# Low parts of layer 2 on VectorE, weight sums among the block products, and weight pieces spread over four periods

## The chip, the core and the metric

One core of a Trainium2 chip runs the whole program. The metric is the device time of one execution in microseconds (us); lower is better. TensorE multiplies (its operands come from SBUF, its sums go to PSUM), VectorE (DVE), ScalarE (ACT) and GpSimd (POOL) work elementwise, and SyncE (SP) issues nearly all DMAs. Each engine takes its instructions strictly in order.

## The reference

Pooled attention, then two mixture-style layers on 2304 tokens of width 512:

```python
x = attention(pooled q, k, v)            # 2304 x 512
h = x @ w1_in;  g = h - tanh(h);            x = g @ w1_out
h = x @ w2_in;  g = h * sigmoid(1.702 * h); out = g @ w2_out
# w_in: 512 x 2048, w_out: 2048 x 512, float64 in memory
```

## The kernel before

**High and low parts.** TensorE multiplies in fp32r. To keep accuracy every operand is split into a high part, a rounded copy that ScalarE makes (`activation(..., Copy)`), and a low part, the value less its high part, which VectorE or GpSimd subtracts. Each product is then three: high x high, high x low, low x high. A low part waits for its high part, and so its engine waits for ScalarE.

**Weights.** Weights come as pieces of 128 x 512 float64, loaded by SP into two alternating buffers `raw` and converted bit by bit: `convert_steps` is `shift` (L137 on ScalarE, L138 on VectorE), `sign` (L144), `flush` (L151) and `tail` (L158) on VectorE, then `split` (high L165 on ScalarE, low L166 on GpSimd). 'i' pieces are of w_in, 'o' pieces of w_out.

**Order.** The schedule is written by hand: lists of jobs are hung on named places (`at(step, place, job)`) and run there, so the program order of each engine's queue is the order in which the places are passed.

**Stages.** Attention runs to about 395 us. `moe` then goes through 50 steps: 40 for layer 1 (four quarters of w_in's columns, five token blocks, two halves each) and steps 40 to 49 for the first quarter of layer 2, the *plain quarter*. A step n issues `h_part(n)` (24 products of 512 or 384 columns into one PSUM tile), `y_part(n - 2)` (products of g and w_out, 18 or 24 a step) and `gate(n)`: `split_g(n - 1)` (high part L1070 on ScalarE, low part L1072), in layer 2 a sigmoid on ScalarE (L1127) and the product h * s on VectorE (L1131), and the accumulations of earlier y (VectorE L1175, ScalarE L1173). Places of a step are "start", "split", "convert", "end". PSUM has four tiles in rotation, so TensorE waits where an older tile has not been read.

In the plain quarter the operands of the rest are prepared beside the steps: `split_x` (L106, L110) for the plain blocks; `combine` (L705) forms sums X1 to X4 of token blocks, `stage` splits them (high L712, low L714) in one of two buffers and sends them to DRAM (L715); `keep` sends raw operands there (L733); `fetch` brings all back later (L737). `prepared` converts w_in pieces and sends them to a home (L759) or splits w_out pieces (L765, L766); `form` combines w_in pieces to sums S1 to S4 (L789) and splits these (high L800, low L803).

`second_layer` does the other three quarters of layer 2 with Winograd-style block products: nine periods i (three quarters by three token groups; a quarter's index s). A period has seven block products of 24 matmuls each (L915, places h0 to h6, PSUM banks a, b, c in turn), each followed by `h_after` (VectorE L927 to L938, which frees banks), the gate (L943, L944), and then the six products of the previous period's g with w_out (L967, places y0 to y5, 12 matmuls each) with accumulations `add` on VectorE (L980). `low_g` (L953) makes the low part of g on GpSimd. w_in pieces of a quarter are formed at y0 of the quarter before; pieces are loaded and converted at the places that `plan` and `loads` give.

Of the kernel before, what the change touches and what calls it, by code (L numbers as in the profile page):

```python
# [9 lines left out]
I32 = mybir.dt.int32  # L10
# [13 lines left out]
def f32(ap):  # L24
    return ap.bitcast(F32)
# [3 lines left out]
def tile_pooled_attention_two_moe(  # L29
# [94 lines left out]
            nc.sync.dma_start(out=raw.rearrange("p (a b) -> p a b", a=shape), in_=src)  # L124
        return raw

    def convert_steps(raw, hi, lo, shape, box, to=None):
        def shift():
            box["t"] = to
            if to is None:  # L130
                box["t"] = wpool.tile([128, DM], I32, tag="wt", name="wt", bufs=2)
            if raw.dtype == F32:
                nc.scalar.activation(f32(box["t"][:]), raw, AF.Copy)
                return
            top = raw[:, :, 1]
            box["a"] = wpool.tile([128, DM], F32, tag="wa", name="wa", bufs=1)
            nc.scalar.activation(box["a"], f32(top), AF.Abs)  # L137
            nc.vector.tensor_scalar(  # L138
                out=box["t"], in0=top, scalar1=3, scalar2=0x3FFFFFF8,
                op0=ALU.logical_shift_left, op1=ALU.bitwise_and,  # L140
            )

        def sign():
            nc.vector.scalar_tensor_tensor(  # L144
                out=box["t"], in0=raw[:, :, 1], scalar=-0x40000000, in1=box["t"],
                op0=ALU.bitwise_and, op1=ALU.bitwise_or,
            )

        def flush():
            t, a = box["t"], box["a"]  # L150
            nc.vector.scalar_tensor_tensor(  # L151
                out=f32(t[:]), in0=a, scalar=2.0 ** -15 * 1.125, in1=f32(t[:]),
                op0=ALU.is_ge, op1=ALU.mult,
            )

        def tail():
            t = box["t"]
            nc.vector.scalar_tensor_tensor(  # L158
                out=t, in0=raw[:, :, 0], scalar=29, in1=t,
                op0=ALU.logical_shift_right, op1=ALU.bitwise_or,  # L160
            )

        def split():
            t = f32(box["t"][:]).rearrange("p (a b) -> p a b", a=shape)
            nc.scalar.activation(hi, t, AF.Copy)  # L165
            nc.gpsimd.tensor_tensor(lo, t, f32(hi), op=ALU.subtract)  # L166

        def nothing():
            pass

        bits = [sign, flush, tail] if raw.dtype == I32 else [nothing] * 3
        return [shift, *bits, split]
# [6 lines left out]
    def piece(kind, n):  # L179

        li, f = divmod(n, NQ * 4)
        if kind == "i":
            src = layers[li][0][f].rearrange("p (c f) -> p c f", c=NKC)
            shape = NKC
        else:
            src = layers[li][1][f * 128:(f + 1) * 128, :].rearrange("p (a d) -> p a d", a=1)
            shape = 1
        box = {}

        def ld():  # L190
            box["raw"] = load_piece(src, shape)

        def cv(j):
            def go():
                if "s" not in box:
                    w = weight(kind, n)
                    hi, lo = ((w[:, :, 0, :], w[:, :, 1, :]) if kind == "i"
                              else (w[:, 0:1, :], w[:, 1:2, :]))
                    box["s"] = convert_steps(box["raw"], hi, lo, shape, box)
                box["s"][j]()  # L200
            return go

        return [ld] + [cv(j) for j in range(5)]
# [432 lines left out]
    def second_layer(mem, HL, work, TEMPS):  # L636
# [73 lines left out]
        def stage(n, o, m):  # L710
            t = stages[m]
            nc.scalar.activation(t[:, 0], shed[o], AF.Copy)  # L712
            eng = nc.vector if o in (X3, X4) else nc.gpsimd
            eng.tensor_tensor(t[:, 1], shed[o], f32(t[:, 0]), op=ALU.subtract)  # L714
            nc.sync.dma_start(out=kept[n][o], in_=whole(t))  # L715

        def keep(n, o):
# [21 lines left out]
        def prepared(kind, qn, f, home=None):  # L739
            n = qn * 4 + f  # L740
            m = n - NQ * 4
            if kind == "i":
                src, shape = layers[1][0][m].rearrange("p (c f) -> p c f", c=NKC), NKC
            else:
                src = layers[1][1][m * 128:(m + 1) * 128, :].rearrange("p (a d) -> p a d", a=1)
                shape = 1
            box = {}

            def ld():
                box["raw"] = load_piece(src, shape)  # L750

            def cv(js):
                def go():
                    if "s" not in box:
                        box["s"] = convert_steps(box["raw"], None, None, shape, box)
                    for j in js:
                        box["s"][j]()
                    if js[-1] == 3 and home is not None:
                        nc.sync.dma_start(out=home, in_=f32(box["t"][:]))  # L759
                return go  # L760

            def split():
                w, t = weight("o", n), f32(box["t"][:]) if home is None else home
                t = t.unsqueeze(1)
                nc.scalar.activation(w[:, 0:1, :], t, AF.Copy)  # L765
                nc.gpsimd.tensor_tensor(w[:, 1:2, :], t, f32(w[:, 0:1, :]), op=ALU.subtract)  # L766

            return [ld, cv((0, 1)), cv((2, 3)), split], box

        def form(qn, fp, boxes, homes):  # L770
# [29 lines left out]
                nc.scalar.activation(w[:, a:b + 1, 0], source(a, b), AF.Copy)  # L800

            def low(a, b):
                nc.gpsimd.tensor_tensor(  # L803
                    w[:, a:b + 1, 1], source(a, b), f32(w[:, a:b + 1, 0]), op=ALU.subtract)

            def run(fn, *args):
# [17 lines left out]
        def early(w, place, *js):  # L824
            opening.extend((w, place, j) for j in js)
# [8 lines left out]
        for qn in range(QN, 2 * NQ):  # L834
# [8 lines left out]
            if s == 0:  # L843
                for n in range(4):
                    early(1 + n, "end", ins[n][0][0])
                    early(3 + n, "convert", ins[n][0][1])
                    early(3 + n, "end", ins[n][0][2])
                early(7, "start", *fs[0])
                early(8, "start", *fs[1])
                for n in range(3):  # L850
                    early(5 + n, "end", outs[n][0])
                    early(7 + n, "convert", outs[n][1], outs[n][2])
                early(7, "end", outs[0][3])
                early(8, "end", outs[1][3], outs[3][0])
                plan = ((outs[3], 0, "h3", "h4"),)
                loads = []
            elif s == 1:
                plan = (
                    (ins[0][0], 1, "h4", "h5"), (ins[1][0], 1, "y1", "y2"),
                    (ins[2][0], 1, "y3", "y4"), (ins[3][0], 2, "h0", "h1"),  # L860
                    (outs[0], 2, "h3", "h4"), (outs[1], 2, "y1", "y2"),
                    (outs[2], 2, "y3", "y4"), (outs[3], 3, "h2", "h3"))
                at(2, "h5", outs[0][3])
                at(2, "y3", outs[1][3])
                loads = list(zip((
                    (0, "h5"), (0, "h6"), (1, "h6"), (1, "y3"), (1, "y5"), (2, "h2"), (2, "h5"),
                    (2, "y3")), (js[0] for js, *_ in plan), strict=True))
            else:
                plan = (
                    (ins[0][0], p, "h5", "h6"), (ins[1][0], p, "y2", "y3"),  # L870
                    (ins[2][0], p + 1, "h0", "h1"), (ins[3][0], p + 1, "h3", "h4"),
                    (outs[0], p + 1, "y1", "y2"), (outs[1], p + 2, "h0", "h1"),
                    (outs[2], p + 2, "h3", "h4"), (outs[3], p + 2, "y2", "y3"))
                at(p + 1, "y4", outs[0][3])
                loads = list(zip((
                    (p, "h0"), (p, "h2"), (p, "h5"), (p, "y3"), (p + 1, "h2"), (p + 1, "h5"),
                    (p + 1, "y3"), (p + 2, "h2")), (js[0] for js, *_ in plan), strict=True))
            for js, i, one, two in plan:
                at(i, one, js[1])
                at(i, two, js[2])  # L880
            for place, job in loads:
                at(*place, job)
            if s > 0:
                if s > 1:
                    at(p + 2, "h5", outs[1][3])
                at(p + 2, "y0", *fs[0], *fs[1])
            q = s * NG
            at(q + 1, "h3", outs[2][3])
            at(q + 1, "h4", outs[3][3])
# [135 lines left out]
    def moe(ctx: ExitStack, ending):  # L1025
# [38 lines left out]
        def split_g(n):  # L1064
            b = steps[n][2]
            at = TEMPS[f"g{n % 2}"]
            gt = mem[:, at:at + 4 * TB].rearrange("p (j r t) -> p j r t", j=2, r=2)
            gt = gt[:, :, :, 0:TBS[b]]
            g = gg.pop(n)
            nc.scalar.activation(gt[:, :, 0, :], g, AF.Copy)  # L1070
            eng = nc.gpsimd if n < len(steps) - 1 else nc.vector
            eng.tensor_tensor(gt[:, :, 1, :], g, f32(gt[:, :, 0, :]), op=ALU.subtract)  # L1072
            gs[n] = gt

# [206 lines left out]
```

## Time and profile before

| | us |
|---|---|
| median of 3 runs | 1204.1 (1200.88 to 1204.54) |
| the profiled execution | 1201.35 |
| its span in the trace | 1199.6 |

| engine | busy us | share of the span |
|---|---|---|
| TensorE matmul | 1180.7 | 98% |
| TensorE weight load | 982.3 | 82% |
| VectorE | 987.5 | 82% |
| ScalarE | 644.0 | 54% |
| GpSimd | 599.6 | 50% |

Busy shares are means over the stages. An engine that waits inside an instruction (for a port or a clock) counts as busy, so a high share alone does not say that it does useful work all that time. The profile has, beside the page with these sums, windows (busy time of each engine in a stretch), timelines, the chain of waits that ended last, and groups of instructions by line.

### The profile page before, as it was taken

To read this page: it belongs to the slowest core of one execution; us is meant where nothing else is said; L and a number is where in the kernel's file an instruction comes from. 1 tells how busy PE (TensorE), PEld (TensorE's weight loads), DVE (VectorE), ACT (ScalarE), POOL (GpSimd) and SP (SyncE) were. 2 spreads that over 40 slices of the span, in tenths; PEclk is the share of its full clock that TensorE was granted. 3 is DMA by queue.
4 is the path that set the end of the run, shared out by engine and by line. 5 is a ranking of instruction groups with operands and counts; after the bars stand their busy time and mean duration, and the time that the engine had idled before them with its cause. 6 is when DMAs were issued, how large, how long until landed. Compare 5 with 4: busy or idle time off the path is not lost. (4 is left out here: it accounts for less than half of the span.)

```text
span 1199.6 us, 23548 instructions
## 1 busy us (share of the span) xinstructions
PE 1180.7 (98%) x9492; PEld 982.3 (82%) x9492; DVE 987.5 (82%) x1115; ACT 644.0 (54%) x955; POOL 599.6 (50%) x388
## 2 busy tenths in 40 slices
PE   9999999999999999999999999998989998999998
PEld 7777676767676888888898898897879997999996
DVE  6788888888888799999999999989975998787442
ACT  4656565656565678676666666664544343333220
POOL 6888888788877323333323323333451354335221
PEclk9999999999999999999999999998999999999999
DMA  4222322233221021110110111113988667665512
GB/s 150 98 89 77 144 82 90 89 122 107 81 81 50 12 63 36 54 53 36 53 53 36 36 53 36 36 36 149 337 330 340 247 238 278 264 229 193 202 41 100
DMA packets 50156, 143.91 MB, mean 120 GB/s; under 512 B 13184, under 2 KB 18816, under 8 KB 50048
## 3 DMA queue, kind: packets, MB, share of 16 engines
q1 hardware_dynamic: 49504, 142.01, 32.7%
q8 instruction: 75, 1.23, 0.4%
q10 hardware_dynamic: 544, 0.39, 0.1%
q14 instruction: 33, 0.27, 0.1%
HBM read 116.13 MB, written 21.31 MB: 115 GB/s over the span
## 5 line engine op out<-in xcount | busy, mean ns | idle before, releaser
L338 DVE TENSOR_REDUCE mt<-mx 128x2 fp32r<-128x1024 f32 (+2 forms) x176 | 195.8, 1136 | 59.9 <-PE mx L326 37.1
L413 POOL TENSOR_TENSOR sum<-sum,pf 128x576 f32<-128x576 f32 x126 | 185.0, 1468 | 9.9
L402 ACT ACTIVATE pf<-sc 128x576 f32<-128x576 f32 x288 | 173.8, 653 | 22.5 <-PE sc L396 10.8
L1155 PE MATMUL y<-mem,big 128*128 128x512 f32 (+1 forms) x780 | 184.8, 368 | 0.9 <-POOL mem L1072 0.9
L1155 PEld LDWEIGHTS y<-mem,big 128*128 128x128 f32 x780 | 142.6, 188 | 20.5 <-POOL mem L1072 1.6
L1072 POOL TENSOR_TENSOR mem<-work,mem 128x1024 fp32r<-128x1024 f32 (+1 forms) x49 | 109.8, 2242 | 87.9 <-ACT mem L1070 87.8
L428 PE MATMUL acc<-pf,v 128*32 128x288 f32 x2304 | 146.3, 407 | 0.0
L1058 PE MATMUL h<-mem,big 128*128 128x512 f32 (+1 forms) x564 | 127.1, 377 | 0.0
L166 POOL TENSOR_TENSOR big<-wt,big 128x512 fp32r<-128x512 f32 x33 | 45.0, 1363 | 161.4 <-ACT big L165 153.3
L428 PEld LDWEIGHTS acc<-pf,v 128*32 128x32 f32 x2304 | 71.6, 110 | 65.7 <-ACT pf L402 4.5
L1058 PEld LDWEIGHTS h<-mem,big 128*128 128x128 f32 x564 | 104.3, 188 | 17.0
L953 POOL TENSOR_TENSOR mem<-work,mem 128x768 fp32r<-128x768 f32 x24 | 46.7, 1959 | 143.1 <-ACT mem L948 131.9
L967 PE MATMUL y<-big,mem 128*128 128x512 f32 x405 | 114.0, 390 | 0.0
L1120 ACT ACTIVATE work<-work 128x1024 f32<-128x1024 f32 (+1 forms) x40 | 39.1, 977 | 107.6 <-DVE work L1118 107.6
L396 PE MATMUL sc<-qh,kh 64*128 64x288 f32 x576 | 91.5, 314 | 0.0
L967 PEld LDWEIGHTS y<-big,mem 128*128 128x128 f32 x405 | 75.9, 188 | 15.6
L445 ACT ACTIVATE u<-acc 128x576 f32<-128x576 f32 x30 | 19.6, 652 | 125.6 <-PE acc L437 125.6
L396 PE MATMUL sc<-row,sel 64*128 64x288 f32 x576 | 85.0, 291 | 0.3 <-ACT row L373 0.3
L396 PE MATMUL sc<-qh,kl 64*128 64x288 f32 x576 | 85.0, 291 | 0.0
L396 PE MATMUL sc<-ql,kh 64*128 64x288 f32 x576 | 84.8, 291 | 0.0
L1058 PE MATMUL h<-mem,w 128*128 128x512 f32 (+1 forms) x376 | 84.7, 377 | 0.0
L1058 PEld LDWEIGHTS h<-mem,w 128*128 128x128 f32 x376 | 69.6, 188 | 11.4
(167 smaller groups left out, 2644.1 us busy)
## 6 DMA issues: line engine op xcount, KB each, us to landing
mem<-x SPq DMA_DIRECT2D x36, 768.0 KB
big<-x SPq DMA_DIRECT2D x27, 768.0 KB
raw<-in_moe_w_in_dram SPq DMA_DIRECT2D x32, 512.0 KB
raw<-in_moe_w_out_dram SPq DMA_DIRECT2D x32, 512.0 KB
v<-in_v_dram SPq DMA_DIRECT2D x16, 576.0 KB
x<-big SPq DMA_DIRECT2D x12, 768.0 KB
kr<-in_k_dram SPq DMA_DIRECT2D x15, 576.0 KB
qr<-in_q_dram SPq DMA_DIRECT2D x15, 576.0 KB
```

The source lines that it names most:

```text
L166: nc.gpsimd.tensor_tensor(lo, t, f32(hi), op=ALU.subtract)
L338: nc.vector.tensor_reduce(out, src, AX.X, ALU.max, negate=True)
L396: nc.tensor.matmul(sc[:, s, 0:HB], w[r], m[r, xs], start=(n == 0), stop=(n == 3))
L402: nc.scalar.activation(pf, sc[:, :, 0:HB], AF.Exp, scale=SCALE)
L413: nc.gpsimd.tensor_add(out, parts[p, x], new)
L428: nc.tensor.matmul(acc[32 * n:32 * n + 32, 0], pairs[p]["v"][:, s, t, 32 * h:32 * h + 32], new[t][:, s, :], start=(t == 0), stop=(t == KT ...
L953: eng.tensor_tensor(g[:, :, 1], halves[n][:, fp], f32(g[:, :, 0]), op=ALU.subtract)
L967: nc.tensor.matmul(y, gts[2 * side + fp][:, j, r, 128 * t:128 * t + 128], wo[:, p, :], start=(k == 0), stop=(k == len(terms) - 1))
L1058: nc.tensor.matmul(hb[:, j, 0:TBS[b]], wi[:, c, w, :], x[r][c], start=(k == 0), stop=(k == 3 * NKC - 1))
L1072: eng.tensor_tensor(gt[:, :, 1, :], g, f32(gt[:, :, 0, :]), op=ALU.subtract)
L1120: nc.scalar.activation(a, u, AF.Relu, bias=-T2)
L1155: nc.tensor.matmul(ys[m][:, 0:w], lhsT, rhs, start=(fp == 0 and not low and j == p == 0), stop=(fp == 1 and low and j == 1))
```

## The change

- The low parts that GpSimd made in the plain quarter go to VectorE: of g (`split_g` for layer 2), of `stage` (X1 and X2; X3 and X4 were there), of 'o' pieces from the third of the plain quarter on (`convert_steps` gets `eng`), of `prepared` and of `form`. `low_g` in the block periods stays on GpSimd, as do layer 1's low parts.
- The weight sums of `form` (L789) move from y0 of a quarter's last period to h2 and h4 of that period; the high and low parts stay at y0.
- The load of the plain quarter's last prepared w_out piece moves from the end of step 48 to that of step 49.
- The conversions of each further quarter's eight pieces are spread from some three periods over four, with other places for their loads and for the splits of the first two 'o' pieces.

```diff
-    def convert_steps(raw, hi, lo, shape, box, to=None):
+    def convert_steps(raw, hi, lo, shape, box, eng=None):
...
-            nc.gpsimd.tensor_tensor(lo, t, f32(hi), op=ALU.subtract)
+            (eng or nc.gpsimd).tensor_tensor(lo, t, f32(hi), op=ALU.subtract)
...
-                    box["s"] = convert_steps(box["raw"], hi, lo, shape, box)
+                    late = nc.vector if kind == "o" and n >= NQ * 4 + 2 else None
+                    box["s"] = convert_steps(box["raw"], hi, lo, shape, box, late)
...
         def stage(n, o, m):
             t = stages[m]
             nc.scalar.activation(t[:, 0], shed[o], AF.Copy)
-            eng = nc.vector if o in (X3, X4) else nc.gpsimd
-            eng.tensor_tensor(t[:, 1], shed[o], f32(t[:, 0]), op=ALU.subtract)
+            nc.vector.tensor_tensor(t[:, 1], shed[o], f32(t[:, 0]), op=ALU.subtract)
...
-                nc.gpsimd.tensor_tensor(w[:, 1:2, :], t, f32(w[:, 0:1, :]), op=ALU.subtract)
+                nc.vector.tensor_tensor(w[:, 1:2, :], t, f32(w[:, 0:1, :]), op=ALU.subtract)
...
             def low(a, b):
-                nc.gpsimd.tensor_tensor(
+                nc.vector.tensor_tensor(
                     w[:, a:b + 1, 1], source(a, b), f32(w[:, a:b + 1, 0]), op=ALU.subtract)
...
-                early(8, "end", outs[1][3], outs[3][0])
+                early(8, "end", outs[1][3])
+                early(9, "end", outs[3][0])
                 plan = ((outs[3], 0, "h3", "h4"),)
                 loads = []
-            elif s == 1:
-                plan = (
-                    (ins[0][0], 1, "h4", "h5"), (ins[1][0], 1, "y1", "y2"),
-                    (ins[2][0], 1, "y3", "y4"), (ins[3][0], 2, "h0", "h1"),
-                    (outs[0], 2, "h3", "h4"), (outs[1], 2, "y1", "y2"),
-                    (outs[2], 2, "y3", "y4"), (outs[3], 3, "h2", "h3"))
-                at(2, "h5", outs[0][3])
-                at(2, "y3", outs[1][3])
-                loads = list(zip((
-                    (0, "h5"), (0, "h6"), (1, "h6"), (1, "y3"), (1, "y5"), (2, "h2"), (2, "h5"),
-                    (2, "y3")), (js[0] for js, *_ in plan), strict=True))
             else:
-                plan = (
-                    (ins[0][0], p, "h5", "h6"), (ins[1][0], p, "y2", "y3"),
-                    (ins[2][0], p + 1, "h0", "h1"), (ins[3][0], p + 1, "h3", "h4"),
-                    (outs[0], p + 1, "y1", "y2"), (outs[1], p + 2, "h0", "h1"),
-                    (outs[2], p + 2, "h3", "h4"), (outs[3], p + 2, "y2", "y3"))
...
+                if s == 1:
+                    plan = (
+                        (ins[0][0], 0, "y1", "y2"), (ins[1][0], 1, "h4", "h5"),
+                        (ins[2][0], 1, "y1", "y2"), (ins[3][0], 1, "y3", "y4"),
+                        (outs[0], 2, "h5", "h6"), (outs[1], 2, "y4", "y5"),
+                        (outs[2], 3, "h2", "h3"), (outs[3], 3, "h5", "h6"))
+                    whens = ((0, "h0"), (0, "h5"), (0, "y3"), (1, "h6"), (1, "y3"), (1, "y5"),
+                             (2, "y1"), (3, "h0"))
+                    ends = (2, "y3"), (3, "h1")
+                else:
+                    plan = (
+                        (ins[0][0], p, "y1", "y2"), (ins[1][0], p, "y3", "y4"),
+                        (ins[2][0], p + 1, "h1", "h2"), (ins[3][0], p + 1, "h4", "h5"),
+                        (outs[0], p + 1, "y2", "y3"), (outs[1], p + 2, "h5", "h6"),
+                        (outs[2], p + 2, "y4", "y5"), (outs[3], p + 3, "h2", "h3"))
...
             if s > 0:
-                if s > 1:
-                    at(p + 2, "h5", outs[1][3])
-                at(p + 2, "y0", *fs[0], *fs[1])
+                at(p + 2, "h2", fs[0][0])
+                at(p + 2, "h4", fs[1][0])
+                at(p + 2, "y0", *fs[0][1:], *fs[1][1:])
...
-            eng = nc.gpsimd if n < len(steps) - 1 else nc.vector
+            eng = nc.gpsimd if steps[n][0] == 0 else nc.vector
             eng.tensor_tensor(gt[:, :, 1, :], g, f32(gt[:, :, 0, :]), op=ALU.subtract)
```

In a line of `plan`, (piece, period, one, two), the first two bit operations of a piece run at place `one` of that period and the last two at `two`; p is the first period of the quarter before.

## Rows read from the trace of the kernel before

**Rows 1.** Windows: us; busy us (count) of PE, PEld, DVE, ACT, POOL; clock; DMA share; GB/s.

```profile
816.90:824.00 7.10, 7.07 (x19) 5.58 (x20) 6.89 (x9) 3.09 (x5) 2.44 (x2) 0.57 0.17 65
...
1007.30:1194.80 187.50, 187.44 (x925) 167.20 (x923) 113.47 (x142) 53.20 (x72) 60.22 (x34) 1.00 0.50 188
...
829.50:906.60 77.10, 73.33 (x331) 61.73 (x329) 64.26 (x71) 40.85 (x62) 37.90 (x19) 0.98 0.91 339
```

**Rows 2.** Chain that ended last, in order of time: start us, us, what.

```profile
900.06 6.49 DMA big<-x
...
940.10 16.36 PE y L967 x72
...
958.57 2.08 PE b L915 x12
```

**Rows 3.** Timeline of TensorE from 808 us: start us, us, what [idle before <-releaser].

```profile
808.16 5.64 PE L1058 MATMUL h<-mem,big 128*128 128x512 f32 x24
816.93 7.20 PE L1155 MATMUL y<-big,mem 128*128 128x512 f32 x18 [3.12 <-DVE xb L1175]
...
883.13 7.35 PE L1155 MATMUL y<-big,mem 128*128 128x512 f32 x24 [1.77 <-DVE work L1131]
...
897.07 0.50 PE L1155 MATMUL y<-w,mem 128*128 128x512 f32 x1 [1.49 <-POOL mem L1072]
...
906.68 2.32 PE L915 MATMUL c<-big,mem 128*128 128x384 f32 x12 [0.59 <-DMA big<-x]
...
993.36 3.91 PE L915 MATMUL c<-big,mem 128*128 128x384 f32 x12 [1.76 <-DVE xb L980]
998.74 2.35 PE L915 MATMUL b<-mem 128*128 128x384 f32 x12 [1.47 <-DVE work L927]
```

**Rows 4.** Timelines of VectorE and GpSimd in the plain quarter.

```profile
832.12 1.28 DVE L110 TENSOR_TENSOR mem<-xb,mem 128x512 fp32r<-128x512 f32 x2
...
840.55 5.15 DVE L110 TENSOR_TENSOR mem<-xb,mem 128x512 fp32r<-128x512 f32 x2
...
840.04 2.31 POOL L714 TENSOR_TENSOR big<-work,big 128x768 fp32r<-128x768 f32 x1 [2.29 <-ACT big L712]
```

**Rows 5.** Line L138 from 804 to 907 us: durations min/median/max in ns.

```profile
L138 DVE TENSOR_SCALAR wt<-raw x9: 410/520/2623, 805.1 to 902.2; 128x512 int32<-128x512 int32 x9
```

**Rows 6.** Timelines of VectorE and GpSimd in the third period.

```profile
986.76 2.76 DVE L158 SCALAR_TENSOR_TENSOR wt<-raw,wt 128x512 int32<-128x512 int32 x1
...
986.14 2.84 POOL L803 TENSOR_TENSOR mem<-work,mem 128x1024 fp32r<-128x1024 f32 x1
```

**Rows 7.** VectorE's groups by line, 804.2 to 907 us: busy us, mean ns | idle before.

```profile
L110 DVE TENSOR_TENSOR mem<-xb,mem 128x512 fp32r<-128x512 f32 x8 | 12.2, 1569 | 0.0
L151 DVE SCALAR_TENSOR_TENSOR wt<-wa,wt 128x512 f32<-128x512 f32 x9 | 10.4, 1153 | 0.5
L138 DVE TENSOR_SCALAR wt<-raw 128x512 int32<-128x512 int32 x9 | 9.5, 1057 | 0.0
...
L1131 DVE TENSOR_TENSOR work<-h,work 128x1024 f32<-128x1024 f32 x6 | 7.3, 1219 | 4.3 <-ACT work L1127 4.3
L158 DVE SCALAR_TENSOR_TENSOR wt<-raw,wt 128x512 int32<-128x512 int32 x9 | 6.2, 692 | 0.3
L714 DVE TENSOR_TENSOR big<-work,big 128x768 fp32r<-128x768 f32 x6 | 5.9, 990 | 2.3 <-ACT big L712 2.3
L705 DVE TENSOR_TENSOR work<-xb 128x768 f32<-128x768 f32 x2 | 4.7, 2344 | 0.0
L1131 DVE TENSOR_TENSOR work<-h,work 128x768 f32<-128x768 f32 x4 | 3.8, 955 | 8.0 <-ACT work L1127 8.0
...
L789 DVE TENSOR_TENSOR work<-big 128x256 f32<-128x256 f32 x2 | 0.8, 418 | 0.0
```

**Rows 8.** GpSimd's groups by line, 806 to 907 us, columns as in rows 7.

```profile
L1072 POOL TENSOR_TENSOR mem<-work,mem 128x1024 fp32r<-128x1024 f32 x6 | 15.4, 2562 | 8.7 <-ACT mem L1070 8.6
L714 POOL TENSOR_TENSOR big<-work,big 128x768 fp32r<-128x768 f32 x6 | 12.7, 2124 | 20.3 <-ACT big L712 20.3
L1072 POOL TENSOR_TENSOR mem<-work,mem 128x768 fp32r<-128x768 f32 x3 | 5.5, 1838 | 5.3 <-ACT mem L1070 5.3
```

More of the change, by code (lines that the diff above doesn't have):

```diff
@@ L125, in load_piece @@
         return raw
-    def convert_steps(raw, hi, lo, shape, box, to=None):
+    def convert_steps(raw, hi, lo, shape, box, eng=None):
         def shift():
-            box["t"] = to
-            if to is None:
-                box["t"] = wpool.tile([128, DM], I32, tag="wt", name="wt", bufs=2)
+            box["t"] = wpool.tile([128, DM], I32, tag="wt", name="wt", bufs=2)
             if raw.dtype == F32:
@@ L853, in second_layer @@
                 early(7, "end", outs[0][3])
-                early(8, "end", outs[1][3], outs[3][0])
+                early(8, "end", outs[1][3])
+                early(9, "end", outs[3][0])
                 plan = ((outs[3], 0, "h3", "h4"),)
                 loads = []
-            elif s == 1:
-                plan = (
-                    (ins[0][0], 1, "h4", "h5"), (ins[1][0], 1, "y1", "y2"),
-                    (ins[2][0], 1, "y3", "y4"), (ins[3][0], 2, "h0", "h1"),
-                    (outs[0], 2, "h3", "h4"), (outs[1], 2, "y1", "y2"),
-                    (outs[2], 2, "y3", "y4"), (outs[3], 3, "h2", "h3"))
-                at(2, "h5", outs[0][3])
-                at(2, "y3", outs[1][3])
-                loads = list(zip((
-                    (0, "h5"), (0, "h6"), (1, "h6"), (1, "y3"), (1, "y5"), (2, "h2"), (2, "h5"),
-                    (2, "y3")), (js[0] for js, *_ in plan), strict=True))
-            else:
-                plan = (
-                    (ins[0][0], p, "h5", "h6"), (ins[1][0], p, "y2", "y3"),
-                    (ins[2][0], p + 1, "h0", "h1"), (ins[3][0], p + 1, "h3", "h4"),
-                    (outs[0], p + 1, "y1", "y2"), (outs[1], p + 2, "h0", "h1"),
-                    (outs[2], p + 2, "h3", "h4"), (outs[3], p + 2, "y2", "y3"))
[L874 to L877, printed above, removed]
@@ new lines, in second_layer @@
+            else:
+                if s == 1:
[13 more added lines that the diff above has]
+                        (outs[2], p + 2, "y4", "y5"), (outs[3], p + 3, "h2", "h3"))
+                    whens = ((p, "h4"), (p, "y1"), (p, "y3"), (p, "y5"), (p + 1, "h3"),
+                             (p + 1, "h6"), (p + 1, "y4"), (p + 2, "y1"))
+                    ends = (p + 1, "y4"), (p + 2, "y3")
+                loads = [(when, js[0]) for when, (js, *_) in zip(whens, plan, strict=True)]
+                at(*ends[0], outs[0][3])
+                at(*ends[1], outs[1][3])
```

## The prediction

> **What bounds the kernel now.** I read the windows first, then TensorE's timeline, then the chain of waits, then VectorE and GpSimd beside each other. TensorE is the limit wherever nothing is late: in the last 187.5 us it is busy 187.44 [rows 1], and the chain runs through its products alone: 72 products of g and w_out in 16.36 us (0.227 us each), 12 block products in 2.08 us (0.173 each) [rows 2]. So every microsecond that TensorE gets back earlier reaches the end in full. What is to be seen in its timeline is where it stops [rows 3]:
> - Plain quarter (layer 2's first quarter, steps 40 to 49). The 24 products that begin at 808.16 are done at 813.6 (24 x 0.227), the next begin at 816.93: 3.3 us, waiting for VectorE's adds. The 18 products that follow take 7.20 us where 18 x 0.227 + 0.16 is 4.25: 2.9 us, with a mean granted clock of 0.57 [rows 1], a mixture of 1.2 and 2.4 GHz, right after an idle stretch. At 883.13 it waited 1.77 (about 1.95 from issue to issue) for VectorE's product at L1131, and the next 24 took 7.35 instead of 5.6: 1.75. At 897.07 it waited 1.49 (1.65) for a low part on GpSimd. Together 3.3 + 2.9 + 1.95 + 1.75 + 1.65 = 11.6 us.
> - First block period: 0.59 (0.76) for the fetch of X3, which took 6.49 us from its issue at 900.06 [rows 2], an issue that stood in SP's queue behind a weight load waiting for a free buffer.
> - Third and fourth period: at 993.36 it waits 1.76 for an accumulation (L980), that product runs 3.91 instead of 2.24, and at 998.74 it waits 1.47 for h_after's L927: from the due time 991.4 to 998.74, less one product of 2.08, 5.2 us.
>
> All of it: 11.6 + 0.8 + 5.2 = 17.6 us. That is the most that the change can win, since it adds and removes no product.
>
> Why VectorE is late there: its operations on two SBUF operands, and L138, stand still while GpSimd works. Two L110 that take 1.28 us at 832.12 take 5.15 at 840.55, half a microsecond behind the start of GpSimd's L714, with its L1072 next in line [rows 4]. L138 takes 0.41 at best and 2.62 at worst [rows 5]. At 986.76 an L158 of 0.69 takes 2.76, beside a GpSimd L803 of 2.84 [rows 6]. Over the plain quarter four groups hold 8 x (1.57 - 0.64) + 9 x (1.15 - 0.69) + 9 x (1.06 - 0.41) + 2 x (2.34 - 0.95) = 7.4 + 4.1 + 5.9 + 2.8 = 20 us of such standing [rows 4, 5, 7]; 0.69 is L158's mean and 0.95 that of an undisturbed 768-column operation, L1131's [rows 7].
>
> **The change, part by part.**
>
> *Plain quarter, low parts to VectorE.* From step 41 on GpSimd gets nothing until the block periods, so the 20 us go. Added to VectorE: nine low parts of g (six of 1024 columns, three of 768) and six low parts in stage (X1 and X2 of three token groups), which are on GpSimd now [rows 8], four weight splits of 512 columns, and two forms of 512 + 1024 + 256 columns. A low part with both operands in SBUF isn't shown at each width; a 768 takes 0.99 (L714), a 512 0.64 (half the L110 pair), 256 columns 0.42 (L789) [rows 4, 7]. For 1024 the bounds are 0.99 (the next narrower) and 1.22 (L1131, same width, one operand in PSUM); I take 1.22. Sum: 6 x 1.22 + 3 x 0.95 + 6 x 0.99 + 4 x 0.64 + 2 x (0.64 + 1.22 + 0.42) = 7.3 + 2.9 + 5.9 + 2.6 + 4.6 = 23.3 us. Against the 20 that go, VectorE's work grows by 3.3 us; it had 4.3 + 8.0 = 12.3 us of waiting for ScalarE in front of L1131 alone [rows 7] to take that up.
>
> Does it keep ahead of TensorE? I lay the queue out step by step, without standing. Consecutive operations overlap by some 0.08 us (two 0.68 in 1.28), so 1024 columns cost 1.14, 768 0.87, 512 0.6, a conversion 0.42 + 3 x 0.66 = 2.4. Step 43, a full one: low part of g 1.14, product 1.14, four pieces of combine 2.0, conversion 2.4, two L110 1.2, two stages 1.74: 9.6. A step of TensorE is 48 x 0.227 = 10.9. Laid out like this steps 41 to 49 are 11.7, 7.4, 9.7, 9.1, 9.2, 6.4, 9.1, 8.9 and 4.3, with 0.9 for the last low part 77 us; step 40 ends at about 810.6, so VectorE could be through at 887. TensorE's own work from 808.16 (144 products of 512 columns and 48 of 384 for h, 180 of 512 for y: 324 x 0.227 + 48 x 0.173) is 81.8 us, to 890.0 instead of 901.5. The margins where TensorE needs VectorE: the four adds of step 41, with 0.87 and 0.6 of low parts now ahead of them, have half done at 813.05 where 813.6 is due; the low part of step 41's g is ready at 823.2, due at 824.0; after that 1 to 6 us. So the stops go, by thin margins at the front. A VectorE instruction that now waits for ScalarE's high part (stage, split, form) holds all behind it; ScalarE for its part waits in stage for the DMA of the piece before last. These waits are what I can't lay out to the microsecond: 0 to 4 us, and I take 2, nearer to the free end because steps 46 and 49 hold 6 us of slack.
>
> *Loads moved.* The load of the last out-weights goes from the end of step 48 to that of 49, behind the fetches of X4, X3 and X22, so X3's issue no longer waits for a buffer: the 0.8 us go if the DMA queues keep up (rival 3).
>
> *Forms.* The eight L789 (8 x 0.34 = 2.7 us of start to start) leave the y stage of a quarter's last period for the h stage, at h2 and h4; the low parts come to VectorE there, 2 x (0.6 + 1.14 + 0.34) = 4.2 us, and GpSimd's L803 go. Behind the two combines wait h_after's adds: h2 to h6 get 2.5, 1.8, 2.4, 1.9 and 2.2 us for slots of 2.08, 0.4 over in all, and the bank that an add has to free is due one to two slots later; so 0.
>
> *Pieces over four periods.* In the y stage of period 2 eight operations of conversion stood among the accumulations, each blocked by L803 or by the low part of g (as in [rows 6]); now there are four, at y4 and y5. The forms' low parts end some 10 us after gating, about 982, the first two accumulations by 984 (due 989), L927 of the next period at about 992 (due 993.5). The 5.2 us go. What is late next is h1 to h3 of period 3 and 4, where a split or a conversion now stands beside GpSimd's low part of g, which stays there: by the same layout L932 ends 12.0 to 12.4 us into the period, due at 12.5. Cost 0 to 1.5 us, inside the 2 above.
>
> **Sum.** 17.6 - 2 = 15.6 us off the profiled execution's 1201.35: 1185.8. The three runs lie from 1200.88 to 1204.54 with the profiled one near the lower end; their median is 2.75 above it. I can't see where in the kernel that comes from; if it is in the stops it goes with them, so I add half, 1.4: 1187.2, say 1187.
>
> **A rule against the change.** With the stops gone the plain quarter's transfers must fit into less time. In 829.5 to 906.6 the 16 DMA engines are 0.91 busy at 339 GB/s [rows 1]: 70 us of work, 26 MB. The Trainium skill's SBUF page (SBUF — State Buffer, "A bandwidth-pool intuition that's wrong") puts the path between HBM and a core at about 358 GB/s; by that, 26 MB are an estimated 73 us, and the stretch would be transfer-bound like rival 3. The trace's mean of 339 at 0.91 busy is 373 at full use, so it shows slightly more than the page.
>
> **Rivals.**
> 1. *Forecast*, the stops go but for some 2 us: 1187. Chance 0.58; 1183 to 1190.
> 2. *ScalarE and VectorE in their fixed order remain the limit of the plain quarter*: VectorE's longest waits were for ScalarE already, and the low parts now wait too. Then the quarter gains only one of its three stops with its slow products, about 5 us, and 5.2 later: 1201.35 - 10 + 1.4 = 1193. Thin margins speak for it, the 12.3 us of slack against. Chance 0.2.
> 3. *Transfers become the bound*: the first stage write can't leave before 821.4 (low part of X1 behind step 41's work). 70 us of work from there end at 891.4, with the gaps that there were (7 us) at 898.4; X3 is due at 890.0 + 4.2 = 894.2. A stop of 4.2 and slow products of about 2 after it, beside the 0.8 that stays: 17.6 - 4.2 - 2 - 0.8 = 10.6 off, 1201.35 - 10.6 + 1.4 = 1192. Chance 0.12.
> 4. *Slower*: the long VectorE operations aren't GpSimd's doing, or come back through something else (DMA writes, ScalarE). Then 23.3 us are added to a queue with 12.3 us to spare: 11 later in the plain quarter, less up to 5 in the periods: 1201.35 + 6 + 1.4 = 1209. It decides from the point where less than 11 of the 20 us come back. Rows 4 speak against it: same operation, with and without GpSimd beside it. Chance 0.05.
> 5. *The edits cancel*, near 1204. Chance 0.05; it would take new stops in periods 3 to 8, where TensorE is now full.
>
> Range for 8 in 10: 1183 (all of 17.6 off 1200.88) to 1196 (cases 2 and 3 with a spread of 3). A measurement can tell about 0.3%, 3.6 us. Faster by more 0.9, within 0.05, slower 0.05.
>
> **What would show it.** GpSimd empty from 806 to about 915; L110 at 0.68 and L138 at 0.42 throughout the plain quarter; TensorE's first block product near 892; clock 1.0 everywhere from 813 on; no wait for L980 or L927 in period 3. Wrong, if L110 or L138 stay long with GpSimd idle (case 4), if TensorE waits for ScalarE's L1070, L712 or L1173 (case 2), or for big<-x at the third block product (case 3).

## The result and the profile after

| | before | after |
|---|---|---|
| median, us | 1204.07 (4 runs, 1200.88 to 1204.54) | 1184.76 (4 runs, 1182.85 to 1185.09) |
| the profiled execution, us | 1201.35 | 1184.88 |
| its span, us | 1199.6 | 1183.1 |

The ratio of the medians is 0.9842 (95%: 0.9822 to 0.9862): 1.6% faster, 19.3 us by the medians and 16.5 by the two spans. The forecast was 1187, with 1183 to 1196 for 8 in 10, and 0.9 on faster.

What to look at first is what TensorE waited for. The list of its waits from 30 us on, before: line, releaser, us in total, times, longest us.

```profile
PE y L1155 <- DVE xb L1175: 3.1, 1, 3.1
PE y L1155 <- POOL mem L1072: 2.9, 4, 1.5
PE y L1155 <- DVE work L1131: 1.8, 1, 1.8
PE c L915 <- DVE xb L980: 1.8, 1, 1.8
PE b L915 <- DVE work L927: 1.5, 1, 1.5
PE acc L437 <- POOL sum L413: 0.6, 1, 0.6
PE c L915 <- DMA big<-x: 0.6, 1, 0.6
```

The same list of after:

```profile
PE y L1155 <- POOL mem L1072: 1.4, 3, 0.6
PE acc L436 <- POOL sum L412: 0.6, 1, 0.6
PE y L1155 <- DVE xb L1175: 0.2, 1, 0.2
```

The 1.4 and one 0.6 are in layer 1 and in attention, which the change doesn't touch. From 808 us on TensorE waits for 0.2 us where it waited for 10.3. The windows of after, columns as in [rows 1], show the same. The first is most of the plain quarter, the second most of the block periods, from within period 3 on (periods are counted from 0):

```profile
829.50:890.00 60.50, 60.50 (x280) 51.47 (x279) 53.91 (x78) 36.22 (x54) 0.00 (x0) 1.00 1.01 383
990.00:1178.00 188.00, 188.00 (x929) 168.22 (x929) 121.83 (x159) 53.45 (x73) 41.55 (x22) 1.00 0.52 190
```

TensorE is busy through, at a granted clock of 1.00, and GpSimd is empty in the plain quarter. The timeline of TensorE there holds one stop, and the first block product, at 901.5 in the working of the prediction, comes at 891.78:

```profile
814.81 4.35 PE L1155 MATMUL y<-big,mem 128*128 128x512 f32 x18 [0.21 <-DVE xb L1175]
...
891.78 2.27 PE L915 MATMUL a<-big,mem 128*128 128x384 f32 x12
```

The first of these is the 7.20 us row of [rows 3]: the same 18 products, 4.35 us at full clock. VectorE's groups of the plain quarter in after answer to [rows 7] (L110 and the lines from L915 on keep their numbers; of those between, L704 and L711 are one lower than before, the others two):

```profile
L712 DVE TENSOR_TENSOR big<-work,big 128x768 fp32r<-128x768 f32 x12 | 11.1, 952 | 3.3 <-ACT big L711 3.3
L1072 DVE TENSOR_TENSOR mem<-work,mem 128x1024 fp32r<-128x1024 f32 x6 | 7.3, 1219 | 0.0
L1131 DVE TENSOR_TENSOR work<-h,work 128x1024 f32<-128x1024 f32 x6 | 7.3, 1218 | 0.0
L149 DVE SCALAR_TENSOR_TENSOR wt<-wa,wt 128x512 f32<-128x512 f32 x10 | 6.9, 687 | 0.5
L110 DVE TENSOR_TENSOR mem<-xb,mem 128x512 fp32r<-128x512 f32 x8 | 5.1, 684 | 0.0
L136 DVE TENSOR_SCALAR wt<-raw 128x512 int32<-128x512 int32 x10 | 5.0, 495 | 0.0
L1131 DVE TENSOR_TENSOR work<-h,work 128x768 f32<-128x768 f32 x4 | 3.8, 952 | 2.6 <-ACT work L1127 2.6
```

L110 is at 684 ns (1569 before), L149 at 687 (1153), L136 at 495 (1057). Nine of the ten L136 take 0.42 us; the tenth, 1.20 us at 805.88, is beside GpSimd's last low part ahead of the block periods (805.50 to 806.80). The 1024-column low part costs 1219 ns, the value taken for it. Between the start of the 18 products above and the first block product lie the same 349 products in both kernels. The window of before, then that of after, columns as in [rows 1]:

```profile
816.93:901.74 84.81, 81.55 (x349) 67.81 (x349) 71.94 (x77) 41.05 (x62) 41.83 (x22) 0.94 0.79 289
814.81:891.78 76.97, 76.87 (x349) 64.69 (x349) 70.16 (x101) 42.53 (x63) 0.00 (x0) 1.00 0.89 336
```

VectorE runs 24 operations more and is busy 1.8 us less: the standing that went was worth more than the work that came. The 12.3 us in which it waited for ScalarE ahead of L1131 are down to 2.6, in a stretch that is 7.8 us shorter.

### The profile page after: what moved, and what is told of

It reads as the page before. It is cut to its first block, busy times and chain, and to the rows that moved or that the text cites. A ratio compares the mean times of both kernels' runs of the same rounds, so it can differ in the third digit from the quotient of the medians.

```text
span 1183.1 us, 23507 instructions
## 1 busy us (share of the span) xinstructions
PE 1172.4 (99%) x9492; PEld 976.4 (83%) x9492; DVE 982.6 (83%) x1162; ACT 644.2 (54%) x955; POOL 514.6 (43%) x341
## 4 chain that ended last, share of the span: by engine, by line
PE 85%; DVE 9%; ACT 3%; POOL 1%; issue 1%; DVEq 0%; POOLq 0%; ACTq 0%
PE y L1155 15%; PE h L1058 14%; PE sc L395 13%; PE y L967 12%; PE acc L427 12%; PE b L915 5%; PE a L915 3%; PE c L915 3%; PE mx L325 3%; PE acc L436 3%; DVE wt L142 1%; DVE work L1101 1%; DVE work L1118 1%; DVE xb L1175 1%; ACT work L1099 1%
## 5 line engine op out<-in xcount | busy, mean ns | idle before, releaser
L1072 POOL TENSOR_TENSOR mem<-work,mem 128x1024 fp32r<-128x1024 f32 (+1 forms) x40 | 89.0, 2226 | 73.9 <-ACT mem L1070 73.9
L164 POOL TENSOR_TENSOR big<-wt,big 128x512 fp32r<-128x512 f32 x27 | 36.6, 1356 | 150.6 <-ACT big L163 150.6
```

## The experiments

Eleven kernels, each against the kernel before on the same chip. "Before" and "after" are the two kernels; an edit is shown against the one it starts from.

**Each half alone.** *eng_only* is before with the low parts on VectorE and nothing moved; *sched_only* is after with the low parts back on GpSimd, so that only the order is new.

```diff
 eng_only, against before (and the same for g, 'o' pieces, prepared)
-            eng = nc.vector if o in (X3, X4) else nc.gpsimd
-            eng.tensor_tensor(t[:, 1], shed[o], f32(t[:, 0]), op=ALU.subtract)
+            nc.vector.tensor_tensor(t[:, 1], shed[o], f32(t[:, 0]), op=ALU.subtract)
             def low(a, b):
-                nc.gpsimd.tensor_tensor(
+                nc.vector.tensor_tensor(
```

```diff
 sched_only, against after (and the same for stage, 'o' pieces, prepared, form)
-            eng = nc.gpsimd if steps[n][0] == 0 else nc.vector
+            eng = nc.gpsimd if n < len(steps) - 1 else nc.vector
```

> The kernel before with only the low parts moved to VectorE; schedule, sums and loads as before. Theory L (VectorE stands still while GpSimd works on SBUF, and taking that work away is what pays): the stops of the plain quarter, 11.6 us, are gone but for 0.5; the stop for X3 (0.8) stays, since the weight load still stands before the fetch; in period 2 VectorE has 2.7 of sums, 4.2 of low parts and eight conversions beside the low part of g, done at about 994 to 996 where 993.5 is due, so 0 to 2.5 of the 5.2 stay. Together 1204 - 11.1 - (2.7 to 5.2) = 1188 to 1190. Rival S (the new places of the pieces and sums are what pays, the engine hardly matters): 1201 to 1204.

> The changed kernel with all low parts back on the engines of before; only the new places of pieces, sums and loads are left. Theory L: the plain quarter's stops stay at 11 to 12 us, X3's 0.8 goes, and of the 5.2 in period 2 to 3 at most 1.5 stay, since only four conversions are left beside GpSimd's low parts of the weights: 1204 - 0.8 - (3.7 to 5.2) = 1198 to 1199.5. Rival S: 1185 to 1190. Rival E (only the engines matter there too): 1203 to 1204.

| | median us | ratio (95%) | less than before, us |
|---|---|---|---|
| eng_only | 1202.15 | 0.9988 (0.9979 to 0.9998) | 1.3 |
| sched_only | 1197.26 | 0.9952 (0.9937 to 0.9967) | 6.1 |
| after | 1184.76 | 0.9842 (0.9822 to 0.9862) | 19.3 |

The halves don't add up: 1.3 and 6.1 alone, 19.3 together. sched_only came slightly below the 1198 to 1199.5 expected of it; eng_only missed its 1188 to 1190 by more than 12 us. It lies where rival S had it, but not for the rival's reason, as its trace shows. The trace says where the low parts' gain went. The plain quarter is nearly clear of stops (0.25 us at 813.65), but the first periods have new ones. TensorE's timeline in eng_only (its lines are two lower than those of before):

```profile
979.50 2.38 PE L913 MATMUL b<-big,mem 128*128 128x384 f32 x12 [1.93 <-DVE xb L978]
983.88 2.38 PE L913 MATMUL c<-big,mem 128*128 128x384 f32 x12 [2.00 <-DVE xb L978]
990.23 4.21 PE L913 MATMUL b<-mem 128*128 128x384 f32 x12 [3.97 <-DVE work L925]
...
1088.81 3.72 PE L913 MATMUL c<-big,mem 128*128 128x384 f32 x12 [4.79 <-DVE xb L978]
```

With the products at 4.21, 3.17 (the next one) and 3.72 us instead of 2.24 that is some 11.5 us between periods 2 and 3 and 6.4 between 5 and 6. VectorE's timeline just before shows the reason: at y0 the weight sums (L787) and their low parts (L801) stand in front of the first accumulation (L978), two of the low parts wait for ScalarE, and the conversions behind it fall beside GpSimd's low part of g (L951, 3.81 us from 974.48):

```profile
965.88 0.42 DVE L787 TENSOR_TENSOR work<-w 128x256 f32<-128x256 f32 x1
...
968.61 1.23 DVE L801 TENSOR_TENSOR mem<-work,mem 128x1024 fp32r<-128x1024 f32 x1 [0.58 <-ACT mem L798]
...
974.31 0.68 DVE L978 TENSOR_TENSOR xb<-xb,y 128x512 f32<-128x512 f32 x1
974.90 1.71 DVE L136 TENSOR_SCALAR wt<-raw 128x512 int32<-128x512 int32 x1
976.65 2.19 DVE L142 SCALAR_TENSOR_TENSOR wt<-raw,wt 128x512 int32<-128x512 int32 x1
```

From 965.88 to 974.31, 8.4 us pass before the first accumulation, which frees a PSUM bank that the next period's products need. In before only the sums stood there, 4.0 us. So the low parts that leave GpSimd need the new order, or the last periods pay for what the plain quarter won.

**Which part of the order.** Each of these undoes one move of after. *sums_back* puts the sums back to y0, *pieces_back* gives the pieces their old places (the lists shown in the change's diff), *load_back* the last load its old place.

```diff
 sums_back
-                at(p + 2, "h2", fs[0][0])
-                at(p + 2, "h4", fs[1][0])
-                at(p + 2, "y0", *fs[0][1:], *fs[1][1:])
+                at(p + 2, "y0", *fs[0], *fs[1])
 pieces_back (and so on, for every piece of s == 1 and s > 1)
-                        (ins[0][0], 0, "y1", "y2"), (ins[1][0], 1, "h4", "h5"),
+                    (ins[0][0], 1, "h4", "h5"), (ins[1][0], 1, "y1", "y2"),
 load_back
-                early(8, "end", outs[1][3])
-                early(9, "end", outs[3][0])
+                early(8, "end", outs[1][3], outs[3][0])
```

> The changed kernel with the sums of the weights back at y0, all else as changed. Theory Q: with the pieces spread VectorE had about 2 us to spare behind its last accumulation of period 2 (L927 waited 1.6 and an accumulation 0.5 for TensorE); the sums and two waits for ScalarE put 2 to 4 us back there, of which the shorter h stage returns some: 0 to 2 us, 1185 to 1187. Rival M: most of the 18 us of the run with the engines alone come back: 1195 to 1202.

> The changed kernel with the pieces at their places of before; low parts on VectorE, sums among the products and the later load are kept. Theory Q (what the run with the engines alone lost, 11.5 us between periods 2 and 3 and 6.4 between 5 and 6, comes from a VectorE queue too long in the y stage of a quarter's last period: sums, low parts and eight conversions that stand beside the low part of g): the sums' 2.8 us and two waits for ScalarE of 0.6 leave that queue, but come back in part through a later gate; 4 to 8 and 2 to 4 us of the stops stay: 1191 to 1197. Rival M (the sums' place is what cured it, not the pieces'): 1185 to 1187. Rival N (the pieces' place alone cured it): 1200 to 1203.

> The changed kernel with the last prepared w_out piece loaded at the end of step 48 again, ahead of the fetches of X4, X3 and X22 in SP's queue. The load waits for a buffer until about 888.2, so X3 leaves at about 889 and lands at 892 to 895.5, where TensorE wants it at 896. Theory Q: 0 to 0.5 us, 1185; the move was worth less than the 0.8 that I gave it, because VectorE is through earlier as well. Rival D (the transfers are the next limit, with the DMA engines full from 829 to 890): X3 lands at 897 to 900 and 1 to 4 us come back with slow products behind them: 1186 to 1190.

| | median us | ratio (95%) | over after, us |
|---|---|---|---|
| sums_back | 1194.6 | 0.9922 (0.9905 to 0.9938) | 9.8 |
| pieces_back | 1192.73 | 0.9905 (0.9891 to 0.992) | 8.0 |
| load_back | 1184.66 | 0.9836 (0.9822 to 0.9851) | -0.1 |
| eng_only: all three back | 1202.15 | 0.9988 (0.9979 to 0.9998) | 17.4 |

The last column compares medians from different chips; by the ratios it would differ by up to 0.8 us. pieces_back came as expected (1191 to 1197), load_back too; sums_back missed (1185 to 1187), its 9.8 us are close to the rival's. Sums and pieces are each worth more than the prediction gave them, and here the parts do add up: 9.8 + 8.0 = 17.8, against 17.4 for all three. The stop of sums_back, TensorE's timeline, comes once between periods 2 and 3 and, as long, between 5 and 6:

```profile
985.23 3.74 PE L913 MATMUL b<-mem 128*128 128x384 f32 x12 [3.62 <-DVE work L925]
...
1083.54 3.21 PE L913 MATMUL b<-mem 128*128 128x384 f32 x12 [3.63 <-DVE work L925]
```

pieces_back has stops of 1.99 and 2.46 us between periods 2 and 3 alone, with two products of 3.9 us behind them. The load's move bought nothing that shows: in load_back X3 is issued at 888.40 and not at 884.05, right behind the load at 887.48, and TensorE takes it at 895.78 without a stop.

**The cause of the long operations.** Rival 4 says that GpSimd isn't the reason. *double_read* is after, where GpSimd computes the nine low parts of g and the six of X1 and X2 once more into an idle tile; *double_write* gives GpSimd, at the same moments, a copy of one column and two fills of that tile instead. Both add work to GpSimd alone.

```diff
 double_read (and the same for each low part of g)
             nc.vector.tensor_tensor(t[:, 1], shed[o], f32(t[:, 0]), op=ALU.subtract)
+            if o in (X1, X2):
+                nc.gpsimd.tensor_tensor(
+                    rbd[:, 0:2 * G].rearrange("p (c t) -> p c t", c=2), shed[o], f32(t[:, 0]),
+                    op=ALU.subtract)
 double_write (and the same for each low part of g)
+            if o in (X1, X2):
+                nc.gpsimd.tensor_copy(rbd[:, 0:1], f32(t[:, 0, 0, 0:1]))
+                for _ in range(2):
+                    nc.gpsimd.memset(rbd[:, 0:2 * G], 0.0)
```

> The changed kernel; in the plain quarter GpSimd subtracts the low parts of g (nine) and of stage (X1, X2: six) a second time into a tile that is idle then, and nothing waits for these results. Theory L: some 34 us of GpSimd work make VectorE stand for 10 to 20 us; its queue of 77 us becomes 87 to 97 against TensorE's 82, and the stops come back: 5 to 15 us, with slow products behind them, 1191 to 1203. Rival P (TensorE waited for GpSimd's slow low parts, not for a VectorE that stood): nothing waits, 1184 to 1186. What decides is the length of VectorE's L110 and L136 beside GpSimd: 1.2 for a pair and 0.41, or 3 to 5 and up to 2.6.

> As double_read, but GpSimd copies one column (to keep the same moments) and then fills the idle tile twice, about as long as the subtraction: it writes SBUF and hardly reads it. Theory L in its narrow form, as the Trainium skill's SBUF page has it (operations of VectorE with two SBUF operands stand only beside a GpSimd operation that reads SBUF; L136, with one operand, beside any): L110, L149, L704 keep 0.64 to 0.95, L136 goes to 1 to 2.5 where it meets a fill; 0 to 3 us, 1184 to 1188. Rival W (any GpSimd work makes VectorE stand): like double_read, 1191 to 1203.

| | median us | ratio (95%) | over after, us |
|---|---|---|---|
| double_read | 1203.92 | 1.0004 (0.9994 to 1.0014) | 19.2 |
| double_write | 1184.26 | 0.9844 (0.9829 to 0.9858) | -0.5 |

Operations whose result nobody reads, on an engine that TensorE and VectorE hardly wait for, take back the whole gain as soon as they read SBUF; fills take nothing. (double_read lies 0.9 us above the range expected of it, double_write inside its range.) TensorE has eight stops again from 818 us on, 14.4 us together, with slow products behind some. Over the same 349 products as above, the window of double_read:

```profile
818.36:911.42 93.06, 82.80 (x349) 67.61 (x349) 88.95 (x98) 39.89 (x59) 31.75 (x12) 0.95 0.76 278
```

VectorE is busy 88.95 us there, 18.8 more than in after, with no operation added to it; in double_write it is 70.7. L136 has a median of 1.20 us instead of 0.42; L110 kept its 0.69. VectorE's timeline in double_read:

```profile
839.25 3.23 DVE L704 TENSOR_TENSOR work<-work,xb 128x256 f32<-128x256 f32 x2 [0.61 <-POOL rbd L714]
842.41 4.87 DVE L704 TENSOR_TENSOR work<-xb,work 128x256 f32<-128x256 f32 x2
```

GpSimd's timeline in double_read (L1078 is the repeated low part of g, L714 that of stage):

```profile
832.53 6.69 POOL L714 TENSOR_TENSOR rbd<-work,big 128x768 f32<-128x768 f32 x1 [9.66 <-ACT big L711]
839.30 2.64 POOL L1078 TENSOR_TENSOR rbd<-work,mem 128x1024 f32<-128x1024 f32 x1
842.02 2.18 POOL L714 TENSOR_TENSOR rbd<-work,big 128x768 f32<-128x768 f32 x1
844.28 2.45 POOL L1078 TENSOR_TENSOR rbd<-work,mem 128x1024 f32<-128x1024 f32 x1
```

A pair of 256-column sums takes 3.23 and 4.87 us beside GpSimd where one such sum takes 0.42 alone. It goes the other way too: at 832.53 GpSimd's operation of about 2.1 us took 6.69 while VectorE ran one operation with two SBUF operands after another, up to 837.4. So rival 4 is out. Another rival would be that GpSimd's repeats hold buffers that others wait for. The only such wait in the list is VectorE's 0.61 us above, too little for 19; ScalarE and SP have none. What double_write can't tell: only one L136 (0.42 us at 890.20) meets fills, and it begins just before one of them ends; the next fill then takes 0.98 us instead of 0.74. Whether a fill holds up an L136 that begins well inside it stays open.

The Trainium skill (SBUF — State Buffer, "Who interferes with whom") says that a VectorE instruction with two SBUF inputs contends with a GpSimd instruction that reads SBUF and not with one that only writes it, and that the one that starts first keeps the other out. Both runs agree with the first part: 19.2 us against -0.5. On the second, the 6.69 us show GpSimd kept out over a whole row of VectorE operations, not over one.

**Which low parts.** *g_back* leaves the plain quarter's low parts of g on GpSimd, *only_g* moves these alone, *form_back* leaves the forms' low parts on GpSimd; all have the new order. *eng_no_form* has the old order and leaves the forms' on GpSimd.

```diff
 g_back, against after (only_g undoes all the others, as sched_only does)
-            eng = nc.gpsimd if steps[n][0] == 0 else nc.vector
+            eng = nc.gpsimd if n < len(steps) - 1 else nc.vector
 form_back, against after; eng_no_form is eng_only with the same
-                nc.vector.tensor_tensor(
+                nc.gpsimd.tensor_tensor(
                     w[:, a:b + 1, 1], source(a, b), f32(w[:, a:b + 1, 0]), op=ALU.subtract)
```

> The changed kernel with the low parts of g of the plain quarter (nine) back on GpSimd; all else as changed. Theory L: VectorE loses 10.2 us of work and stands some 8 to 10 beside 21 us of GpSimd; its queue stays as long as it is, 77, so no stop of VectorE's making comes back, but the low parts come later (2.5 instead of 1.2 us), which the margins of 1 to 6 us take except at the front (0.8): 0 to 3 us, 1185 to 1188. Rival G (the low parts of g are the heart of the change): 8 us or more come back, 1193 to 1197.

> The changed kernel with only the low parts of g on VectorE; those of stage, weight splits and forms are back on GpSimd (some 28 us of GpSimd in the quarter). Theory L: VectorE loses 13.1 us of work and stands 8 to 12 beside GpSimd; no net change in the quarter, 0 to 3 us, and 0 to 1 in the periods as with the forms' low parts alone: 1185 to 1188. Rival G: 1184 to 1186, no stop at all. Rival O (stage, splits and forms are the heart): 1193 to 1197.

> The changed kernel with only the low parts of the formed weights (L803 before) back on GpSimd. Theory Q: VectorE gets 4.2 us back at y0 and stands some 2 to 4 us beside 11 us of GpSimd there, where only four conversions are left; the low part of g behind them comes 5 us later, still before it is wanted: 0 to 1 us, 1185 to 1186. Rival F (these low parts on GpSimd were what held period 3 in the kernel before): 4 to 8 us come back, 1189 to 1193.

> The kernel before with the low parts of g, of stage and of the weight splits on VectorE; the low parts of the formed weights stay on GpSimd, the schedule is that of before. It asks why the run with the engines alone gained nothing. Theory Q (the form's 4.2 us of low parts with their two waits for ScalarE, put into VectorE's queue at y0 ahead of the accumulations, turned the 5.2 us of the kernel before into 11.5 and 6.4): the quarter's 11.6 us and X3's 0.8 go, the 5.2 between periods 2 and 3 stay and periods 5 to 6 are as before: 1204 - 12.4 = 1190 to 1193. Rival (TensorE's coming 12 us earlier, or anything else of the quarter's moves, is what made the periods worse): 1198 to 1203.

| | median us | ratio (95%) | TensorE's stops |
|---|---|---|---|
| sched_only: none moved | 1197.26 | 0.9952 (0.9937 to 0.9967) | 3.15, 2.31, 3.08 and a slow product, 0.25, 0.8 |
| only_g | 1188.45 | 0.9885 (0.9869 to 0.9902) | 2.4 (adds) and a slow product, 0.8 |
| g_back | 1187.18 | 0.9868 (0.9853 to 0.9883) | 1.0, 0.75, 1.4 (L1131) |
| form_back | 1186.8 | 0.9851 (0.9836 to 0.9866) | 0.5, 0.2 |
| after: all moved | 1184.76 | 0.9842 (0.9822 to 0.9862) | 0.2 |
| eng_no_form | 1197.67 | 0.9958 (0.9943 to 0.9973) | 2.4 (X3), 6.3 (L978) and slow products, 0.6, 0.3, 0.2 |

With the new order, the low parts of g alone win 8.8 of the 12.5 us, and all the others without g 10.1: either half takes away most of the stops, and only after, with both, is down to 0.2. The intervals of form_back and g_back overlap after's, so their prices aren't clear of noise; for g_back the trace has 3.2 us of stops. g_back came as expected, only_g and form_back lie 0.5 and 0.8 us above their ranges, and the rivals G, O and F, at 1193 or more, are out.

eng_no_form missed what was expected (1190 to 1193). Its two long stops, in TensorE's timeline, are of two kinds:

```profile
899.46 3.82 PE L913 MATMUL c<-big,mem 128*128 128x384 f32 x12 [2.37 <-DMA big<-x]
...
992.19 4.21 PE L913 MATMUL c<-big,mem 128*128 128x384 f32 x12 [6.30 <-DVE xb L978]
```

The DMA issue on SP that belongs to the first:

```profile
892.39 0.36 SPq L735 DMA_DIRECT2D big<-x  x1
```

This is X3: its issue stood behind the weight load, which waited for a buffer until 891.46. So the load's old place does cost, as soon as VectorE's conversion is late; in load_back it isn't. The load's move is a margin here and no gain. The second stop: from y0 of period 2 on, GpSimd's low parts, of the forms up to 985.0 and of g after that, stand beside the conversions on VectorE. Among these is an 'o' piece's low part (L164), which the change put there. VectorE's timeline in eng_no_form:

```profile
976.75 2.05 DVE L136 TENSOR_SCALAR wt<-raw 128x512 int32<-128x512 int32 x1
...
981.68 2.77 DVE L156 SCALAR_TENSOR_TENSOR wt<-raw,wt 128x512 int32<-128x512 int32 x1
984.37 0.67 DVE L978 TENSOR_TENSOR xb<-xb,y 128x512 f32<-128x512 f32 x1
985.15 2.23 DVE L164 TENSOR_TENSOR big<-wt,big 128x512 fp32r<-128x512 f32 x1
987.31 2.03 DVE L136 TENSOR_SCALAR wt<-raw 128x512 int32<-128x512 int32 x1
...
991.46 0.67 DVE L978 TENSOR_TENSOR xb<-xb,y 128x512 f32<-128x512 f32 x1
```

The fourth accumulation comes at 991.46, 15.3 us after the first (976.15). With the old order the y stage of period 2 is overfull with the forms' low parts on either engine: 8.4 us ahead of the accumulations on VectorE, or standing among them beside GpSimd.

## Why the prediction was right, point by point

- **The sum of the stops, 17.6 us: right.** The plain quarter's first products begin at 808.16 before and at 808.96 after, which is 0.8 lost ahead of what the change touches. It is lost in attention's first 17 us (1.0 us there, 0.2 comes back later): the first products that wait for ScalarE's L373 begin at 15.94 before and at 16.97 after (there L372), and in after TensorE waits 2.0 us at 9.18 for ScalarE, in before not at all there. The edits don't reach that place, and the wait differs among the runs that share them: 1.57 us in load_back, none in double_write. From the first products to the end of the span it is 391.4 us before and 374.1 after: 17.3 us gained.
- **The residual, 2 us: too large.** By the same count it is 0.3, and the list of waits shows 0.2. VectorE's waits for ScalarE's high parts are there (3.3 us ahead of L712), and all of them lie in VectorE's slack. The 3.3 us by which VectorE's work was to grow didn't come either: it is busy 1.8 us less.
- **Margins in the plain quarter: the right places, slightly too wide.** The tightest was the first one, the adds of step 41, forecast at 0.5 us to spare; they came 0.2 too late, which is the one stop that is left. The first block product was laid out for 890.0, counted from 808.16; it came at 891.78, counted from 808.96: 1.0 us later than laid out.
- **X3, 0.8 us: gone, but by another edit.** The stop goes because VectorE's conversion ends earlier; with the load in its old place it stays away (load_back, -0.1).
- **Pieces and forms, 5.2 us and 0: the forecast of the whole held, but their value was mis-sized.** The 5.2 are gone: the L927 at 980.91 now waits for TensorE. But I counted the sums' move at no gain. The low parts that come to VectorE at y0 would bring new stops of some 17 us between periods 2 and 3 and 5 and 6, and the moves take these away too (sums 9.8, pieces 8.0). The prediction laid out the new order as a whole, with the low parts at y0 in it, and that held; its price for each move looked at what the move takes out of before, not at what the other edit would put there.
- **Half of the gap between median and profile, 1.4 us: not settled.** Medians differ by 19.3 us and spans by 16.5, so the added gain had the right sign; where in the kernel the rest comes from isn't shown.

Of the rivals, the fourth fell with double_read. The second, ScalarE and VectorE in their fixed order, needs stops that aren't there. The fifth, edits that cancel through new stops from period 3 on, is what eng_only shows; the new order keeps it from after. The third, transfers as the bound, shows no stop, but the transfers do fill 829.5 to 890.0, with a share of 1.01 at 383 GB/s, and ScalarE waited for the buffer of a stage write. In after's timeline of ScalarE:

```profile
863.97 0.84 ACT L711 ACTIVATE big<-work 128x768 fp32r<-128x768 f32 x1 [4.70 <-DMA x<-big]
```

This 4.7 us wait reaches nobody that TensorE waits for. How much more traffic the quarter would bear wasn't tried. The Trainium skill's figure of about 358 GB/s between HBM and a core (SBUF — State Buffer, "A bandwidth-pool intuition that's wrong") is below the 383 measured over 60 us of loads and stores together; by the measurement the stretch is full, and TensorE still has no stop for it.

## What to carry to other kernels

When VectorE's two-operand operations vary by a factor of two to four, look at what GpSimd reads at that moment: operations moved from GpSimd to VectorE can cost less than nothing there (1.8 us less here), and fifteen that GpSimd ran "for free" cost 19 us. But work that is moved to the busier engine lands in its queue wherever that job is called, so lay out every place where it is called, not only the stretch that was slow; 17 of the 19 us depended on clearing two such places, the y stages of periods 2 and 5. An edit that is worth nothing when undone alone (the load) may still be the margin of another one.

## What the runs showed of the hardware

The exclusion works both ways, and a small operation can suffer most: in double_write GpSimd's copy of a single column took 1.47 us in the mean behind stage and 0.55 behind the gate, while fills of 768 columns ran in 0.74. The longest copy, the last line below, ended at 831.94, as VectorE's row of operations with two SBUF operands came to its end (831.89); the shortest copy took 0.18.

```profile
L716 POOL MEMSET rbd<- 128x768 f32 x12 | 8.9, 742 | 0.7
L714 POOL COPY rbd<-big 128x1 f32<-128x1 f32 x6 | 8.8, 1468 | 21.6 <-ACT big L711 21.5
L1078 POOL COPY rbd<-mem 128x1 f32<-128x1 f32 x9 | 5.0, 552 | 22.9 <-ACT mem L1074 22.7
...
826.88 5.06 POOL L714 COPY rbd<-big 128x1 f32<-128x1 f32 x1 [8.13 <-ACT big L711]
```

And a stop costs more than its length. Windows over single groups of 12 products (x13 where a neighbour reaches in) in eng_only, columns as in [rows 1]: the group behind 1.93 us of idle (the first stop between periods 2 and 3), the one behind the 3.97 us, and the next one.

```profile
979.50:981.80 2.30, 2.30 (x12) 2.06 (x12) 2.16 (x4) 1.00 (x2) 0.00 (x0) 1.00 0.01 2
990.20:994.30 4.10, 4.08 (x13) 4.08 (x14) 1.99 (x3) 0.00 (x0) 0.00 (x0) 0.50 0.96 380
994.30:997.20 2.90, 2.90 (x13) 2.90 (x12) 2.62 (x4) 0.20 (x1) 0.00 (x0) 0.67 0.41 170
```

At a granted clock of 0.50, the lower level of 1.2 GHz, the 12 products take 4.1 us instead of 2.24, and the clock comes back only within the next group. Not every stop does it: behind idle stretches of about 2 us the group ran at 1.00 in eng_only, and took 3.9 us in pieces_back. The 18 products behind the 0.21 us stop of after kept the full clock, at 4.35 us.
